# Row groups of 8 and 4 for the reversed loads, angles in turns by integer rounding, chunk C of the first batch later, and two narrower tiles, in a fused Fourier mixing and SwiGLU kernel

## The chip, the cores and the metric

The kernel runs on one core of a Trainium2 chip. The metric is the device time of one execution in microseconds (us), and the figure of a kernel is the median of its runs. Before the change it was 713.37 us in three runs (713.21 to 714.16). A program on one core has no other cores to be compared with. Its runs are called fast when they lie within 1.5% of the fastest run of the same kernel.

The engines are named as in the profile: PE is the matrix engine, PEld its weight loads, DVE the vector engine, ACT the scalar engine (activations and copies), POOL the general engine (GpSimd), and SP the queue that issues most transfers.

## The reference

```python
def _attn_ref(x):                       # x: (8, 3008, 256)
    X = np.fft.fft(x, axis=1)
    X = np.fft.fft(X, axis=2)
    return X.real.astype(np.float32)

def _moe_ref(x, w_gate, w_val, w_out):  # x: (24064, 256), weights 256 x 1536 and 1536 x 256
    g = x @ w_gate
    silu = g * (1.0 / (1.0 + np.exp(-g)))
    val = x @ w_val
    return (silu * val @ w_out).astype(np.float32)
```

The output of the first function, as 24064 rows of 256, is the input of the second.

## The kernel before

The kernel uses the symmetry of a real transform: it makes the cosine part P and the sine part Q of each batch for half of the columns, and gets one output row from P + Q and its mirror from P - Q. So the main loop has "plus halves" (`part_a`) and "minus halves" (`part_b`). A tile is up to 512 columns, a unit is one tile and one of 12 blocks of 128 hidden features, and tile t begins at unit 12t.

For each batch the input rows come in two chunks, A (128 rows) and C (60 rows and one more), each with ascending ("up") and descending ("down") rows. For batches 1 to 7 the POOL engine folds them into coefficients (`CEa`, `BBa`, `CEc`, `BBc`), and PE transforms the coefficients. The first batch is different, because PE has nothing else to do: the rows of one direction are put in order by a product with a permutation (`place`), DVE adds and subtracts (`sums`), ACT copies to bf16 (`halves`), and PE multiplies without the folds (`unfolded`). The other half of the first batch's columns, the job (0, 1), is done with folds at unit 9.

```python
    T = 512
    nT = (NC + T - 1) // T                    # NC = 8 * 1504 columns
    ...
    LA, NA = 16, P // 16                      # chunk A: 8 groups of 16 rows
    LC, NC_ = 15, NCR // 15                   # chunk C: 4 groups of 15 rows
    ...
    def up_block(b, j, n):
        return rows_at(b, 2 * j - 1, [[2 * D, n], [R * D, 4], [1, 2 * D]])
    def down_set(b, a, j, L, n):
        return rows_at(b, R * (a + 1) - 2 * j, [[2 * L * D, n], [-2 * D, L], [1, 2 * D]])
    def load_a(b, q):                         # batches 1 to 7
        X3 = XA.rearrange("p a q d -> p a (q d)")
        return ([lambda h=h: q.dma_start(out=X3[LA * h:LA * (h + 1), 0:4, :],
                                         in_=up_block(b, JA - LA * h, LA)) for h in range(NA)] +
                [lambda a=a: q.dma_start(out=X3[:, 4 + a, :], in_=down_set(b, a, JA, LA, NA)) for a in range(4)])
    ...                                       # the start; temporaries of two pools that are released together:
    SA = tp.tile([P, 2, 4, 2, D], F32, name="SA")
    SC = tq.tile([P, 2, 2, 2, D], F32, name="SC")
    ...
    psA = place(XA, putA, 4, ((psG, "g"), (psV, "v")))
    sums(SA, 0, XA, psA)
    halves(SBa, SA, 0)
    clear(XC, 1)                              # ACT
    sums(SA, 1, XA, psA)
    halves(SBa, SA, 1)
    psC = place(XC0, putC, 2, ((psO, "o"),))  # PE: waits for chunk C's rows
    unfolded(0, 0, SBa, True, False)          # PE: chunk A's products
    ...
    for q in range(2):                        # POOL: folds of the first batch, chunk A then C
        ...
            pts(dst, src, scalar1=sgn, scalar2=sg, op0=Alu.mult, op1=Alu.mult)   # BBc, the last read of SC
    ...
    transform(0, 0, (0, 1), acc)
    tmp_ctx.close()                           # all the temporaries' memory becomes free for the main loop
    hp = ctx.enter_context(tc.tile_pool(name="ht", bufs=2))
    sgp = ctx.enter_context(tc.tile_pool(name="sg", bufs=3))                     # Silu's outputs
    ...
            if k:                             # in transform_w, per block of weights
                nc.scalar.copy(dst[:, gv, fs], ps)
                nc.scalar.activation(Wm[:, gv, fs], ps, AF.Copy, scale=m2)       # ACT
```

## Time and profile before

| | before |
|---|---|
| median of three runs | 713.37 us |
| span of the profiled run | 709.6 us, PE clock 0.984 of full |
| PE busy | 672.3 us, 95% |
| POOL busy | 581.6 us, 82% |
| first product of the main loop | 39.30 us |
| start of job (0, 1), unit 9 | 65.18 us |
| start of job (2, 1), unit 76 | 224.89 us |

The page of the kernel before: its first lines, and from the slices (40 of 17.7 us; each digit is the busy share in tenths) those of PE, POOL and the PE clock.

```profile
span 709.6 us, 13046 instructions
PE 672.3 (95%) x4293; PEld 413.7 (58%) x4363; DVE 520.0 (73%) x932; ACT 439.9 (62%) x762; POOL 581.6 (82%) x563
...
PE   4678999998999999999999999999999999999997
POOL 7995889999898989999799889999699854654610
PEclk9699999999999999999999999999999999999999
```

PE is full from the fifth slice on, but for one at about 160 us. So only the start, the stretch to 200 us and the tail can give anything. The windows of the kernel before (stretch in us; its length; busy time of PE, PEld, DVE, ACT and POOL, with instructions; PE clock; share of the 16 DMA engines; GB/s):

```profile
16.00:23.70 7.70, 0.00 (x0) 0.00 (x0) 2.37 (x5) 7.62 (x5) 7.25 (x13) 0.50 0.62 115
...
58.00:62.00 4.00, 1.91 (x9) 0.68 (x7) 3.66 (x5) 1.63 (x3) 3.84 (x6) 1.00 1.10 133
...
100.00:120.00 20.00, 19.83 (x129) 12.62 (x129) 15.69 (x25) 13.23 (x24) 17.68 (x18) 1.00 0.23 77
140.00:160.00 20.00, 18.44 (x119) 11.60 (x120) 15.27 (x25) 12.65 (x22) 19.92 (x20) 1.00 0.18 57
160.00:180.00 20.00, 16.73 (x102) 9.21 (x102) 11.96 (x28) 8.38 (x15) 18.54 (x19) 0.91 0.57 137
200.00:320.00 120.00, 118.89 (x755) 72.56 (x767) 91.47 (x157) 75.77 (x133) 113.82 (x104) 1.00 0.28 73
```

From 140 to 180 us PE loses 4.8 of 40 us while POOL is busy 38.5 of 40: PE waits there for POOL's late work. The waits are 1.4 us at 159.8 for POOL's product `hp`, 0.95 us at 164.1 for a buffer `vv` that POOL frees, and 1.8 and 0.3 us at 169.7 for the coefficients of batch 2. (The profile names ACT for the 1.8 us, but POOL's `CEa` ends at 169.64, just before PE goes on.) The two longest waits of PE (waits view: engine, tile and line, what it waited for; us in all, times, longest):

```profile
PE o L380 <- ACT SBa L394: 13.9, 1, 13.9
PE o L448 <- ACT Wm L432: 3.1, 1, 3.1
```

The first is put down to ACT, but line 380 is `place`, and the tile in it is chunk C's. The timeline shows what happens (start, us, engine, line, instruction, and in brackets the idle time just before and what ended it):

```profile
23.76 3.75 PE L380 MATMUL o<-XC_106,putC 128*128 128x512 f32 x4 [13.89 <-ACT SBa L394]
39.30 0.39 PE L703 MATMUL g<-Pt,Wp 128*128 128x512 bf16 x1 [0.73 <-DVE Pt L572]
39.34 0.50 POOL L501 TENSOR_SCALAR BBc<-SC,sgn 128x1 bf16<-128x1 f32 x2
40.52 0.60 ACT L730 ACTIVATE sg<-g 128x512 f32<-128x512 f32 x1 [1.75 <-PE g L703]
73.02 4.67 POOL L148 TENSOR_TENSOR SDf<-XA 128x1024 f32<-128x1024 f32 x2 [10.32 <-DMA XA<-in_x_dram]
```

The placement of chunk C stands in PE's queue ahead of chunk A's products, and its rows come late, so PE is idle from 9.9 to 23.8 us and its clock falls to 0.50 (first window above). The Trainium skill, "TensorE: Matmul & The Clock Gate", section "What's actually happening", says that the halved clock is the default state and comes back after an idle window of about 3.4 us. The trace of this wait is compatible with that: by the same view the clock was still 1.00 from 12 to 14 us, 0.78 from 14 to 16, and 0.50 after.

### The profile page before, as it was taken

How to read it: one execution, taken by the hardware profiler on the slowest of the kernel's cores; microseconds unless marked ns; L12 is line 12 of the kernel's file. 1: busy time of each engine (PE TensorE's matmuls, PEld its weight loads, DVE VectorE, ACT ScalarE, POOL GpSimd, SP SyncE). 2: the span in 40 equal slices, each digit the busy share in tenths (PEclk: the TensorE clock that was granted, in tenths of full speed). 3: DMA queues.
4: the chain of work that ended last, by engine and by line, in shares of the span. 5: the costliest groups of instructions: out<-in, count | busy, mean ns of one | idle time of the engine just before them, and what ended most of it. 6: DMA issues, size and time to landing. Idle time of an engine off the chain costs nothing.

```text
span 709.6 us, 13046 instructions
## 1 busy us (share of the span) xinstructions
PE 672.3 (95%) x4293; PEld 413.7 (58%) x4363; DVE 520.0 (73%) x932; ACT 439.9 (62%) x762; POOL 581.6 (82%) x563
## 2 busy tenths in 40 slices
PE   4678999998999999999999999999999999999997
PEld 3333656554665656656566556656566556656686
DVE  7378667775777787777787777777877777777762
ACT  6566656563665656656666566656666566666663
POOL 7995889999898989999799889999699854654610
PEclk9699999999999999999999999999999999999999
DMA  6727471516116214206114311115211111111112
GB/s 193 137 35 133 118 161 40 135 44 149 46 45 124 71 30 108 95 30 164 31 46 87 107 31 46 45 31 124 70 46 46 30 45 31 45 45 31 46 51 70
DMA packets 44984, 52.57 MB, mean 74 GB/s; under 512 B 5676, under 2 KB 32884, under 8 KB 44916
## 3 DMA queue, kind: packets, MB, share of 16 engines
q1 hardware_dynamic: 41732, 49.38, 26.8%
q0 software_dynamic: 3184, 2.36, 2.4%
q8 instruction: 34, 0.56, 0.3%
q14 instruction: 34, 0.28, 0.1%
HBM read 29.43 MB, written 24.65 MB: 76 GB/s over the span
## 4 chain that ended last, share of the span: by engine, by line
PE 73%; POOL 8%; issue 4%; DMA 3%; DVE 3%; SPq 1%; ACT 1%; POOLq 0%; ACTq 0%
PE o L665 29%; PE v L703 15%; PE g L703 12%; PE g L740 7%; POOL SDf L148 3%; PE v L740 3%; PE g L556 3%; DMA XA<-in_x_dram 3%; PE v L556 2%; DVE vv L722 2%; POOL hp L723 1%; POOL EOf L155 1%; DMA XC<-in_x_dram 1%; DVE vv L720 1%; POOL EOf L151 1%
## 5 line engine op out<-in xcount | busy, mean ns | idle before, releaser
L723 POOL TENSOR_TENSOR hp<-sgv,vv 128x512 bf16<-128x512 f32 x126 | 161.1, 1281 | 62.5 <-DVE vv L720 46.7
L745 POOL TENSOR_TENSOR hm<-sgv,vv 128x512 bf16<-128x512 f32 x126 | 160.9, 1280 | 17.4 <-ACT sgv L744 16.1
L665 PE MATMUL o<-Wo,hp 128*128 128x256 bf16 (+1 forms) x1140 | 170.2, 273 | 2.4 <-POOL hp L723 1.4
L665 PE MATMUL o<-Wo,hm 128*128 128x256 bf16 x1128 | 168.2, 273 | 0.0
L665 PEld LDWEIGHTS <-hp 128*128 128x128 bf16 (+1 forms) x1140 | 111.4, 98 | 71.4 <-issue 9.5
L665 PEld LDWEIGHTS <-hm 128*128 128x128 bf16 x1128 | 110.2, 98 | 63.6 <-issue 3.9
L718 DVE SCALAR_TENSOR_TENSOR es<-bc,w_85,v 128x512 f32<-128x512 f32 x126 | 93.9, 746 | 55.8 <-PE v L703 55.8
L731 DVE TENSOR_TENSOR hp<-sg,v 128x512 bf16<-128x512 f32 (+1 forms) x162 | 107.7, 665 | 33.9 <-ACT sg L730 32.2
L748 ACT ACTIVATE sg<-g 128x512 f32<-128x512 f32 (+1 forms) x162 | 94.6, 584 | 47.3 <-PE g L740 44.1
L730 ACT ACTIVATE sg<-g 128x512 f32<-128x512 f32 (+1 forms) x162 | 94.3, 582 | 45.6 <-PE g L703 42.1
L749 DVE TENSOR_TENSOR hm<-sg,v 128x512 bf16<-128x512 f32 (+1 forms) x162 | 107.1, 661 | 19.8 <-ACT sg L748 11.5
L703 PE MATMUL v<-Pt,Wp 128*128 128x512 bf16 (+1 forms) x287 | 108.0, 376 | 2.7 <-issue 0.2
L703 PE MATMUL g<-Pt,Wp 128*128 128x512 bf16 (+1 forms) x287 | 108.1, 377 | 0.7 <-DVE Pt L572 0.7
L740 PE MATMUL g<-Qt,Wm 128*128 128x512 bf16 (+1 forms) x288 | 108.1, 375 | 0.0
L744 ACT ACTIVATE sgv<-g 128x512 f32<-128x512 f32 x126 | 75.5, 599 | 48.1 <-PE g L740 42.9
L715 ACT ACTIVATE sgv<-g 128x512 f32<-128x512 f32 x126 | 75.3, 597 | 43.3 <-PE g L703 16.8
L720 DVE SCALAR_TENSOR_TENSOR vv<-v,es 128x512 f32<-128x512 f32 x126 | 87.2, 692 | 18.1 <-POOL hp L723 1.5
L703 PE MATMUL g<-Qt,Wq 128*128 128x512 bf16 (+1 forms) x240 | 90.0, 375 | 0.6 <-DVE Qt L572 0.3
L722 DVE SCALAR_TENSOR_TENSOR vv<-v,es 128x512 f32<-128x512 f32 x126 | 85.9, 682 | 4.8 <-POOL hm L745 4.3
L703 PEld LDWEIGHTS <-Wp 128*128 128x128 bf16 x576 | 56.5, 98 | 45.1 <-issue 7.9
L671 ACT COPY ev<-o 128x512 f32<-128x512 f32 x94 | 55.1, 586 | 32.6 <-PE o L665 30.9
L148 POOL TENSOR_TENSOR SDf<-XA 128x1024 f32<-128x1024 f32 x28 | 66.1, 2363 | 10.4 <-DMA XA<-in_x_dram 10.3
(179 smaller groups left out, 745.4 us busy)
## 6 DMA issues: line engine op xcount, KB each, us to landing
out_dram<-ev SPq DMA_DIRECT2D x96, 128.0 KB
XA<-in_x_dram SPq DMA_DIRECT2D x32, 256.0 KB
XA<-in_x_dram SPq DMA_DIRECT2D x56, 128.0 KB
XC<-in_x_dram SPq DMA_DIRECT2D x56, 120.0 KB
XA<-in_x_dram SPq DMA_DIRECT2D x1, 1024.0 KB
out_dram<-ev SPq DMA_DIRECT2D x8, 120.0 KB
out_dram<-ev SPq DMA_DIRECT2D x8, 112.0 KB
out_dram<-ev SPq DMA_DIRECT2D x8, 104.0 KB
```

The costliest lines, as they stand in the source:

```text
L665: nc.tensor.matmul(ps[:n, j, :], hts[minus][:, f, c:c + n], Wo[:, f, :], start=(f == 0), stop=(f == nF - 1))
L703: nc.tensor.matmul(ps[:, :w], Wt[:, gv, fs], src[:, :w], start=start, stop=stop, skip_group_check=True)
L718: stt(es, bc[t], w0[:, f:f + 1], e, op0=Alu.mult, op1=Alu.add)
L720: stt(vp, o, -0.5, es, op0=Alu.mult, op1=Alu.add)
L722: stt(vm[:, ::-1], o, 0.5, es, op0=Alu.mult, op1=Alu.add)
L723: nc.gpsimd.tensor_tensor(hts[t][0][:, f, :w], sg, vp, op=Alu.mult)
L730: nc.scalar.activation(sg[:, :w], g[:, :w], AF.Silu)
L731: nc.vector.tensor_tensor(hts[t][0][:, f, :w], sg[:, :w], v[:, :w], op=Alu.mult)
L740: nc.tensor.matmul(ps[:, :w], Wm[:, gv, f * P:(f + 1) * P], Qt[:, :w], start=False, stop=True, skip_group_check=True)
L745: nc.gpsimd.tensor_tensor(hts[t][1][:, f, :], sg, v, op=Alu.mult)
L748: nc.scalar.activation(sg[:, :w], g[:, :w], AF.Silu)
L749: nc.vector.tensor_tensor(hts[t][1][:, f, w - 1::-1], sg[:, :w], v[:, :w], op=Alu.mult)
```

## The change

The intent is a shorter start, and less waiting for the folds later:

- Row groups of 8 (A) and 4 (C) in place of 16 and 15, so that the down rows of the first batch have 16 and 15 groups.
- Angles are counted in turns: POOL rounds by writing an integer, which takes away one pass per table, and some clears and weights of DVE and ACT go.
- A's products stand ahead of C's placement.
- `Wm` is made by POOL, from `Wq`, instead of by ACT.
- Tiles 0 and 3 have 480 columns, so that batches 0 and 1 end with a tile, and batch 1's and 2's transforms are needed 12 units later; the folds are spread anew.

```diff
+    wide = [H - 2 * T, T, T] * 2
+    wide += [T] * ((NC - sum(wide)) // T)
+    if sum(wide) < NC:
+        wide.append(NC - sum(wide))
...
-    LA, NA = 16, P // 16
-    LC, NC_ = 15, NCR // 15
+    LA, NA = 8, P // 8
+    LC, NC_ = 4, NCR // 4
...
     def turns(...):
-            pts(t1[:, i, :], kf[:, lo:hi], scalar1=mM[...], scalar2=BIG, op0=Alu.mult, op1=Alu.add)
-        pts(t1, t1, scalar1=-BIG, scalar2=-float(M), op0=Alu.add, op1=Alu.mult)
+            pts(t1[:, i, :], kf, scalar1=mM[...], scalar2=1.0, op0=Alu.mult, op1=Alu.mult)   # t1 is int32
...
     def weigh(lo, hi):
-        for i in range(2):
-            vts(Tab[:, 1, i, :, lo:hi], Tab[:, 1, i, :, lo:hi], scalar1=wC[:, i:i + 1], ...)
+        vts(Tab[:, 1, 1, :, lo:hi], Tab[:, 1, 1, :, lo:hi], scalar1=wC, ...)
...
-                nc.scalar.activation(Wm[:, gv, fs], ps, AF.Copy, scale=m2)
+                pts(Wm[:, gv, fs], dst[:, gv, fs], scalar1=m2, scalar2=1.0, op0=Alu.mult, op1=Alu.mult)
...
     sums(SA, 0, XA, psA)
     halves(SBa, SA, 0)
-    clear(XC, 1)
+    d_tables()
     sums(SA, 1, XA, psA)
+    unfolded(0, 0, SBa, True, False)
     halves(SBa, SA, 1)
+    ...                                    # tables of chunk C
     psC = place(XC0, putC, 2, ((psO, "o"),))
-    unfolded(0, 0, SBa, True, False)
...
-    spread(("C", 1), 14, 1, 10)
-    spread(("A", 1), 14, 11, slot[(1, 0)] - 1)
+    spread(("C", 1), 14, 1, 12)
+    spread(("A", 1), 14, 13, 24)
+    lo = 25
     for b in range(2, B, 2):
         u = slot[(b, 0)] - 1
-        lo = max(u - 43, slot[(1, 0)])
-        spread(("C", b), 14, lo, lo + (u - lo) // 2)
-        spread(("A", b), 14, lo + (u - lo) // 2 + 1, u)
-        spread(("A", b + 1), 14, u + 6, u + 28)
+        spread(("C", b), 14, lo, (lo + u) // 2)
+        spread(("A", b), 14, (lo + u) // 2 + 1, u)
+        lo = min(u + 26, slot[(b + 1, 0)] - 2)
+        spread(("A", b + 1), 14, u + 2, lo)
+        lo += 1
...
-              4: [..., lambda: value_rows((1, 2))],
+              8: [lambda: value_rows((1, 2))]}
-    for i in range(4):                     # clears of XC on DVE at units 3 to 6
-        before[3 + i].append(lambda i=i: nc.vector.memset(XC...[32:64, ...], 0.0))
...
-        if i == 5:
+        if i == 9:
             loads.extend((("A", 1), fn) for fn in load_a(1, nc.sync))
```

## The prediction

> **What bounds it now.** Page: span 709.6 us, PE busy 672.3 (95%), POOL 581.6 (82%). Stage table: from 200 to 700 us PE is busy 99 of every 100 us at clock 1.00, so only the start can give much. PE idles 16 us in 0-40 (and about 5 us of its busy time there is warm-up on zeros), 8 in 40-100, 5.4 in 100-200, 4 in the tail.
>
> Start, timeline: the placement of chunk C's rows stands in PE's queue ahead of chunk A's products; PE waits 13.9 us in one piece (9.9 to 23.8, waits view), then runs at clock 0.5. First main-loop product 39.3. Units 1-4 are bound by ACT (two 0.6 us Silu, 0.59 + 0.69 us weight copies, a 0.92 us table); PE waits 3.1 us and goes cold once more; unit 5's minus half runs at 56.8. XA for batch 1 is issued at 53.4, lands at 72.5; POOL idles 10.3 us for it. The 100-200 loss is POOL: batches 2's folds are late (waits at 159-170 us, 6 us with the cold clock after them).
>
> **Removed, moved, added.**
> - A's products, placement of C afterwards; XC0 cleared early, down rows of batch 0 in 16 and 15 row groups instead of 8 and 4. The Trainium skill, "DMA: Bandwidth & Descriptors", section "Why a DMA increments its semaphore by 16 and not by 1", says the number of engines must divide the outermost sizes; the trace agrees in kind: 378 GB/s while the one-piece up block lands, 188 after. Later batches swap the two directions, so no gain there, but 20 issues instead of 12 (0.3-0.6 us each on SP), hidden.
> - The 3.6 us clear between the halves copies leaves ACT; the rounding loses one POOL pass of 0.83 us per chunk, twice in the start and twice later.
> - Estimated from these durations: sums of A at 9 (13.6), A's products at 14 (27.3), first unit at 27.5 us (39.3): 12 us earlier.
> - But POOL now makes Wm (0.67 us each, six), and is the next limit: A's and C's remaining folds take 16 us on POOL (23.9 to 39.9) and still start at about 24.5. They end near 40.5; then Wm, two 2.35 us folds of batch 1, the second Wm at about 47. Unit 5 needs it, PE gets there near 39. I expect a PE wait of 6-8 us on POOL and a cold clock after it (about 1.7 us). Unit 5's minus half: about 47-48, so 8 us of the 12 remain.
> - Batch 1 is needed one tile later (unit 33, not 21), batch 2 at 64 instead of 52: the waits of 95 and 159-170 us should shrink (6-8 us). POOL pays: batch 3's and 4's folds are squeezed into units 65-123 (POOL need about 141 us, PE about 140), so some 3-4 us of waits may come back before batch 4 (unit 124).
> - Last tile 320 columns instead of 256: one more output block, 12 x 0.11 = 1.3 us.
>
> **Sum.** 8 + 7 - 3.5 - 1.3 = 10 us: 703.4 us, range 697.5 to 709. Faster by over 2% (below 699.1): 0.2; within 2%: 0.78; slower: 0.02.
>
> **What would show it.** A's products start near 14 us with no 13.9 us wait; first unit near 27-29; a PE wait of several us on POOL's Wm near 40-47; little PE idle at 160-175; POOL over 95% busy from 90 to 320 us; last output block train 72 products.
>
> **What would make it wrong.** Wm on POOL not stalling unit 5 (then under 699); the integer output or conversion slower on POOL; chunk C's rows landing late behind the other loads; XC of batch 2 late behind 40 issues, with POOL waiting; POOL lag from units 65-123 stalling PE by more than 5 us (then 708 or more).

## The result

| | before | after |
|---|---|---|
| median of four runs of each, same chip | 713.29 us (710.33 to 714.16) | 704.34 us (703.65 to 707.96) |
| ratio of the fast runs | | 0.9892, 95% interval 0.9848 to 0.9936 |
| span of the profiled run | 709.6 us | 702.1 us, PE clock 0.99 |

A ratio here is the mean time of one kernel's fast runs over that of the other's of the same rounds, so it is not quite the ratio of the medians quoted. The kernel is 1.1% faster. The time lies 0.9 us from the predicted one. The steps on the way to it were not all right, and that is the subject of the rest.

The page and the windows of the kernel after:

```profile
span 702.1 us, 13265 instructions
PE 676.2 (96%) x4375; PEld 415.8 (59%) x4375; DVE 513.6 (73%) x919; ACT 432.7 (62%) x759; POOL 581.0 (83%) x567
...
PE   7659998999999999999999999999999999999997
POOL 7888789999999999999998989998899645645600
PEclk9979999999999999999999999999999999999999
```

```profile
10.00:16.00 6.00, 3.39 (x12) 1.48 (x12) 5.53 (x10) 4.72 (x7) 5.83 (x11) 0.72 1.13 232
...
58.00:66.00 8.00, 8.00 (x43) 4.02 (x42) 7.14 (x15) 5.78 (x11) 7.84 (x9) 1.00 0.49 103
...
100.00:120.00 20.00, 17.37 (x117) 10.13 (x116) 13.51 (x30) 9.67 (x19) 19.27 (x17) 1.00 0.67 146
140.00:160.00 20.00, 19.90 (x133) 12.76 (x132) 15.52 (x26) 13.56 (x25) 19.92 (x19) 1.00 0.39 114
160.00:180.00 20.00, 20.00 (x133) 13.07 (x131) 14.89 (x23) 13.41 (x25) 19.92 (x20) 1.00 0.20 56
200.00:320.00 120.00, 119.63 (x769) 72.48 (x767) 90.99 (x157) 76.00 (x133) 118.03 (x110) 1.00 0.28 75
```

The loss of 140 to 180 us is gone, with POOL just as busy. A new one stands at 100 to 120 us. In the first 40 us PE has the busy first slice that was wanted, and then a hole: the second and third digits are 6 and 5. The waits of PE name it:

```profile
PE g L742 <- ACT sg L732: 11.9, 2, 10.0
PE v L705 <- DVE vv L724: 2.4, 1, 2.4
```

And the timeline of the kernel after, from the first products to the folds of batch 1:

```profile
12.26 0.50 PE L419 MATMUL v<-Tab,SBa 128*128 128x377 bf16 x1 [2.15 <-ACT SBa L394]
27.63 0.38 PE L705 MATMUL g<-Pt,Wp 128*128 128x480 bf16 x1 [1.15 <-DVE Pt L577]
40.77 0.56 PE L742 MATMUL g<-Qt,Wm 128*128 128x480 bf16 x1 [10.00 <-ACT sg L732]
53.27 0.36 PE L742 MATMUL g<-Qt,Wm 128*128 128x480 bf16 x1 [1.87 <-ACT sg L732]
...
40.15 0.57 ACT L732 ACTIVATE sg<-g 128x480 f32<-128x480 f32 x1 [13.46 <-POOL BBc L505]
...
39.61 0.50 POOL L505 TENSOR_SCALAR BBc<-SC,sgn 128x1 bf16<-128x1 f32 x2
46.83 0.69 POOL L433 TENSOR_SCALAR Wm<-Wq,m_89 128x512 bf16<-128x512 bf16 x1
74.91 4.67 POOL L152 TENSOR_TENSOR SDf<-XA 128x1024 f32<-128x1024 f32 x2 [7.56 <-DMA XC<-in_x_dram]
```

The first product of the main loop starts at 27.63 us, 11.7 us earlier, as predicted. Then nothing follows from it: the Silu of unit 0 starts at 40.15, against 40.52 before. ACT has stood idle for 13.46 us, and what ended it was POOL's `BBc` at line 505. That instruction makes coefficients of the first batch, and Silu does not read them. PE finishes the plus halves of units 0 and 1 and then waits 10.00 us.

How the gain grows and shrinks is best seen at the starts of the batches' transforms on PE (timeline), which stand at the same unit in both kernels (the expectations below call such a start the job's "anchor"):

| job, unit | before | after | gain |
|---|---|---|---|
| (0, 1), unit 9 | 65.18 | 59.95 | 5.2 |
| (1, 1), unit 40 | 136.26 | 132.56 | 3.7 |
| (2, 1), unit 76 | 224.89 | 214.29 | 10.6 |
| (4, 0), unit 124 | 335.83 | 325.22 | 10.6 |
| (7, 1) | 636.40 | 625.85 | 10.55 |
| end | 709.6 | 702.1 | 7.5 |

Part of these gains is only lent. Tiles 0 and 3 are 32 columns narrower and the last tile is 64 wider. In the timeline 512-wide products in a row start 0.215 us apart, and a tile takes about 72 of them (six in each of 12 units, a few less where blocks are split). So 32 columns make an estimate of 0.215 x 32/512 x 72 = 0.97 us per narrow tile, some 1.9 us for both, which the last tile gives back. Taking that out: the start gave about 4.5 us, the stretch to unit 40 lost 2.1, the stretch to unit 76 gave 6.3, nothing happened from there to job (7, 1), and the tail cost about 1.2 more.

### The profile page after: what moved, and what is told of

The parts are those of the page before. It is cut to its first block, busy times and chain, and to the rows that moved or that the text cites. A ratio compares the mean times of both kernels' runs of the same rounds, so it can differ in the third digit from the quotient of the medians.

```text
span 702.1 us, 13265 instructions
## 1 busy us (share of the span) xinstructions
PE 676.2 (96%) x4375; PEld 415.8 (59%) x4375; DVE 513.6 (73%) x919; ACT 432.7 (62%) x759; POOL 581.0 (83%) x567
## 4 chain that ended last, share of the span: by engine, by line
PE 89%; DVE 4%; POOL 3%; issue 2%; DMA 1%; ACT 1%; SPq 0%; DVEq 0%; ACTq 0%; POOLq 0%
PE o L667 34%; PE v L705 17%; PE g L705 16%; PE g L742 9%; PE v L742 4%; PE g L561 3%; PE v L561 3%; DVE vv L724 2%; DMA XA<-in_x_dram 1%; DVE vv L722 1%; PE g L837 1%; PE o L428 1%; PE v L419 1%; PE v L567 1%; PE g L567 1%
## 5 line engine op out<-in xcount | busy, mean ns | idle before, releaser
L725 POOL TENSOR_TENSOR hp<-sgv,vv 128x512 bf16<-128x512 f32 (+1 forms) x126 | 160.5, 1275 | 52.5 <-DVE vv L722 37.5
L747 POOL TENSOR_TENSOR hm<-sgv,vv 128x512 bf16<-128x512 f32 (+1 forms) x126 | 160.2, 1274 | 14.8 <-ACT sgv L746 14.3
L667 PE MATMUL o<-Wo,hp 128*128 128x256 bf16 (+2 forms) x1140 | 169.7, 273 | 0.0
L667 PE MATMUL o<-Wo,hm 128*128 128x256 bf16 (+2 forms) x1140 | 169.6, 273 | 0.0
L667 PEld LDWEIGHTS <-hp 128*128 128x128 bf16 (+2 forms) x1140 | 111.9, 98 | 68.1 <-issue 7.8
L667 PEld LDWEIGHTS <-hm 128*128 128x128 bf16 (+2 forms) x1140 | 111.9, 98 | 64.3 <-issue 4.4
L732 ACT ACTIVATE sg<-g 128x512 f32<-128x512 f32 (+2 forms) x162 | 94.4, 583 | 57.0 <-PE g L705 42.7
L750 ACT ACTIVATE sg<-g 128x512 f32<-128x512 f32 (+2 forms) x162 | 94.7, 584 | 44.4 <-PE g L742 43.6
L742 PE MATMUL g<-Qt,Wm 128*128 128x512 bf16 (+2 forms) x288 | 108.3, 376 | 11.9 <-ACT sg L732 11.9
L746 ACT ACTIVATE sgv<-g 128x512 f32<-128x512 f32 (+1 forms) x126 | 75.3, 598 | 48.1 <-PE g L742 38.7
L717 ACT ACTIVATE sgv<-g 128x512 f32<-128x512 f32 (+1 forms) x126 | 75.1, 596 | 43.4 <-PE g L705 34.0
L722 DVE SCALAR_TENSOR_TENSOR vv<-v,es 128x512 f32<-128x512 f32 (+1 forms) x126 | 87.0, 690 | 18.5 <-POOL hp L725 1.7
L724 DVE SCALAR_TENSOR_TENSOR vv<-v,es 128x512 f32<-128x512 f32 (+1 forms) x126 | 85.6, 679 | 6.2 <-POOL hm L747 3.3
```

Source lines behind the costliest of these rows:

```text
L667: nc.tensor.matmul(ps[:n, j, :], hts[minus][:, f, c:c + n], Wo[:, f, :], start=(f == 0), stop=(f == nF - 1))
L722: stt(vp[:, :w], o[:, :w], -0.5, es[:, :w], op0=Alu.mult, op1=Alu.add)
L724: stt(vm[:, w - 1::-1], o[:, :w], 0.5, es[:, :w], op0=Alu.mult, op1=Alu.add)
L725: nc.gpsimd.tensor_tensor(hts[t][0][:, f, :w], sg[:, :w], vp[:, :w], op=Alu.mult)
L732: nc.scalar.activation(sg[:, :w], g[:, :w], AF.Silu)
L742: nc.tensor.matmul(ps[:, :w], Wm[:, gv, f * P:(f + 1) * P], Qt[:, :w], start=False, stop=True, skip_group_check=True)
```

## The experiments

All twelve ran correctly. In every list of waits, line numbers are of that kernel (the kernels with moved memory are up to five lines longer). "After" is the kernel after, 704.34 us and ratio 0.9892. Each run's ratio is to runs of the kernel before on the same chip, whose median was 711.62, 712.52 and 712.82 us; two kernels are compared through these ratios.

The theory at the start: the Silu of unit 0 waits because its output lies in memory that was released with all the first batch's temporaries at once (`tmp_ctx.close()`), and the last reader of all these temporaries is POOL's `BBc`. The rival is the prediction's own: POOL makes `Wm` too late, and the wait on unit 0 is only where it shows.

### e1: the temporaries not in the way

`SC` and `SA` are put into memory that is not released: `SC` lies over POOL's fold buffer, which is idle then, and `SA` over the buffer of the odd tiles' products, which is used first by tile 1.

```diff
+    HT1 = const.tile([P, nF * (2 * T + B)], BF16, name="HT1")
...
-    SA = tp.tile([P, 2, 4, 2, D], F32, name="SA")
+    SA = HT1[:, 0:8192].bitcast(F32).rearrange(...)    # HT1: odd tiles' hp and hm, always there
...
-    SC = tq.tile([P, 2, 2, 2, D], F32, name="SC")
+    SC = SDf.rearrange("p k (a q) d -> p k a q d", a=2)
...
-    hp = ctx.enter_context(tc.tile_pool(name="ht", bufs=2))
+    hp = ctx.enter_context(tc.tile_pool(name="ht", bufs=1))    # even tiles only
...                                                    # part_a takes HT1 for the odd tiles
```

> Kernel after, but the two temporaries that POOL reads last (the sums of A and of C) lie in memory that is not given back before the main loop (C's in the fold buffer, A's in the second h buffer). Nothing else is changed. Theory 1: the 10 us wait of PE at unit 1 is unit 0's Silu waiting for the release of the temporaries' memory, whose last reader is POOL's BBc at 40.1 us. Then unit 0's Silu starts near 29 us (40.15 in after), the 10 us wait is gone, and the wait I forecast appears instead: unit 4's minus half waits for POOL's second Wm until 47 to 48 us (53.3 in after). Span 702.1 falls to 696-699. Rival A: what is gained at the start is given back before unit 64, because POOL's folds of batches 1 and 2 are what counts from 75 to 190 us: start as in theory 1, span 701-702.5. Rival B: the wait has another cause (PSUM, PE's queue): Silu of unit 0 stays at 40.

Measured: 703.61 us (702.93 to 704.89), ratio 0.9881 (0.9823 to 0.9939). The waits of PE, then the timeline of PE at unit 4 and of POOL at batch 1, and the window in which batch 1's load moves:

```profile
PE v L747 <- POOL Wm L434: 4.9, 1, 4.9
PE v L710 <- DVE vv L729: 4.8, 3, 2.4
```

```profile
47.30 0.58 PE L747 MATMUL v<-Qt,Wm 128*128 128x480 bf16 x1 [4.89 <-POOL Wm L434]
...
73.94 4.66 POOL L153 TENSOR_TENSOR SDf<-XA 128x1024 f32<-128x1024 f32 x2 [7.71 <-DMA out_dram<-ev]
...
52.00:60.00 8.00, 7.95 (x42) 4.07 (x42) 7.05 (x15) 5.61 (x11) 7.76 (x9) 1.00 0.47 74
```

The 10 us wait is gone: Silu of unit 0 runs at 29.10, and job (0, 1) starts at 54.31 instead of 59.95. So the release of these two temporaries was the cause of that wait, and this is shown. (Whether Silu waits for all the temporaries or only for those whose bytes it takes, e1 does not separate.) Behind it comes the wait that had been predicted, on POOL's `Wm`, until 47.30 us, the very time of the prediction ("at about 47"). In the kernel after the same `Wm` comes just as late (46.83 in its timeline), but PE is later still, so it shows as no wait.

And yet the time did not move. Job (1, 0) starts at 114.73 us, against 114.86 in after: all of the 5.6 us are given back in 60 us. POOL is idle for 7.71 us and begins to fold batch 1's chunk A at 73.94, against 74.91 in after. From there to job (1, 0) POOL is nearly full (busy 38.7 of the 40 us from 80 to 120), and PE comes to wait for it: it is busy 33.4 of these 40 us, against 37.3 in after (the longest waits are 2 us at 99 and 2.4 us at 107, on `vv`, whose buffers POOL frees).

Why does POOL start hardly earlier? The load of batch 1 was issued at 51.96 us, 5.6 us earlier than in after (57.60), but its first blocks then moved at 74 GB/s (the window above) instead of 103 (58 to 66 us in after), and so POOL got its rows only 1 us earlier. Why the same blocks moved more slowly is not known. The profile names a store, `out_dram`, as what ended POOL's wait; that it was the load is shown by e5 below.

### e2 and e3: Wm by ACT again, without and with e1

```diff
-                pts(Wm[:, gv, fs], dst[:, gv, fs], scalar1=m2, scalar2=1.0, op0=Alu.mult, op1=Alu.mult)
+                nc.scalar.activation(Wm[:, gv, fs], ps, AF.Copy, scale=m2)
```

> Kernel after, with Wm copied by ACT from PSUM as before, instead of by POOL. Theory 1: POOL's BBc ends 1.4 us earlier, so unit 0's Silu starts near 38.7 instead of 40.15; units 1 to 4 get 0.7 us longer on ACT, about 2.5 us in all, so the second PE wait is larger; net within 1.5 us of after (702.1). If Wm on POOL had been the limit that I forecast (at unit 4), the span would fall by 5 us or more.

Measured for e2: 706.8 us (704.39 to 709.88), ratio 0.9929 (0.9862 to 0.9995). So it is about 0.4% slower than after by the ratios, not faster as it would have to be if `Wm` on POOL were the limit; the difference is within the intervals of both.

> Both edits. Theory 1: no PE wait above 2 us between 28 and 60 us; unit 4's minus half at 40-43 us (53.3 in after). If only the start counts the span is about 691-693. Rival A (POOL's folds take it back by unit 64): PE waits of several us turn up between 75 and 190 us and the span is 696-700, no better than with the first edit alone.

Measured for e3, which is e1 and e2 together: 701.31 us (700.14 to 701.92), ratio 0.9844 (0.9787 to 0.9901), 2.3 us below e1 on the same chip. Job (0, 1) starts at 52.98 and job (1, 0) at 112.19, and no wait of PE on POOL's `Wm` is left.

The same edit is worth nothing, or a loss, while the release stands in the way, and a gain of 2.3 us when it does not. The rival, that `Wm` on POOL is what bounds the kernel after, falls with e2. Why e2 is rather slower is argued and not shown: when ACT may start only at about 40 us, the copies fall into the stretch where ACT has most to do.

### e5: e1 with batch 1's loads three units earlier

e1 pointed to the load. The weights' raw values lie in `XA`, and the load of batch 1 can only be queued after their last reader, `value_rows((1, 2))`, at unit 8.

```diff
               5: [lambda: weigh(NOO, NTAB)],
-              8: [lambda: value_rows((1, 2))]}
+              5: [lambda: weigh(NOO, NTAB), lambda: value_rows((1, 2))]}
-        if i == 9:
+        if i == 6:
             loads.extend((("A", 1), fn) for fn in load_a(1, nc.sync))
```

> The first edit (temporaries not given back early) and, besides, batch 1's chunk A loaded earlier: the value rows of the last two weight chunks, which hold its memory, at unit 5 instead of 8, and the loads from unit 6 instead of 9. Theory 2: in the first run the 6 us gained at the start were lost because POOL waited 7.7 us (until 73.9 us) for these loads, and its late folds then held the products of tile 2. Then POOL's wait goes, its fold of chunk A of batch 1 starts near 67 (73.9), batch 1's transform is at 108-111 instead of 114.7, and the span is 696-699. Rival A: POOL's work up to unit 64 is the limit whatever it starts with, and the span stays at 701-702.5.

Measured: 697.49 us (697.38 to 697.82), ratio 0.9779 (0.9733 to 0.9826). Job (0, 1) is where e1 has it (54.86), and job (1, 0) comes at 108.32 instead of 114.73. The fold of batch 1 in the timeline:

```profile
66.90 4.68 POOL L153 TENSOR_TENSOR SDf<-XA 128x1024 f32<-128x1024 f32 x2 [0.39 <-POOL BBc L172]
```

POOL now goes from chunk C to chunk A without a gap, 7.0 us earlier than in e1, and all or nearly all of it reaches the end (6.1 us by the medians, 6.4 by the profiled spans, about 7 by the ratios). So the gain of e1 had been lost to POOL's wait for batch 1's load, and this too is shown.

### e11: the earlier loads alone

> The kernel after with only the earlier loads of batch 1 (issued from unit 6, the memory they go to freed at unit 5), no memory moved. e5 against e1 gave 6.1 us for this step when unit 0 was not held. If POOL's idle time before batch 1 (7.56 us) is what counts and it starts from the load: loads issued near 52 to 54 instead of 57.6, POOL idle 3 to 5 us, anchor of (1,0) 3 to 4 us earlier (111 to 112), time 700 to 702. If the two steps only pay together: within 1 us of after (703.5 to 705).

Measured: 700.84 us (700.16 to 701.91), ratio 0.9834 (0.9801 to 0.9867). Job (1, 0) starts at 111.12, and POOL's gap is 3.68 us instead of 7.56. Against after, by the ratios, e1 alone gives about 0.8 us, e11 alone 4.1, and both (e5) 8.1 (by the medians, 0.7, 3.5 and 6.9). The intervals are 2 to 4 us wide to each side, so the times alone do not show that the two are worth more together than apart; job (1, 0) shows it, which comes 0.1, 3.7 and 6.5 us earlier than in after. They help each other: freeing unit 0 moves PE forward, and that is kept only if POOL's work comes forward as well.

### e8 and e12: all three, and one thing more

e8 is e3 with the loads of e5.

> All three edits: temporaries kept, Wm on ACT, loads from unit 6. Theory 2: against the run with the first two (699.9) POOL's wait for batch 1's loads goes and the span falls by 3-6 us to 694-697; batch 1's transform at 106-109 (112.2). Rival A: span 699-700.

Measured: 695.47 us (694.4 to 695.68), ratio 0.9748 (0.9709 to 0.9788): faster by over 2%, and the best with e12. Job (0, 1) starts at 52.44, (1, 0) at 105.84, (2, 0) at 176.82.

e12 is e8 without the split blocks in tile 2. A split block makes plus and minus halves on POOL and saves PE a product.

```diff
-        return 2 <= u[0] < nT - 1 and u[1] in SPLIT
+        return 3 <= u[0] < nT - 1 and u[1] in SPLIT
```

> e8 with tile 2 not split into plus and minus halves in the split blocks, which takes about 15 us of work off POOL in units 24 to 35 and adds about 1.3 us of PE products. If POOL is still the limit around 80 to 120 us (PE waits on DVE vv and on hp there): the waits at 97 to 112 go, anchor of (1,0) 2 to 4 us earlier than e8's 105.84, (2,0) at 173 to 176 against 176.82, time 692 to 694.5 against 695.5. If it is the load of batch 1 alone: 695.5 to 697.

Measured: 695.0 us (694.12 to 696.56), ratio 0.9753 (0.972 to 0.9786). That is e8's time. The windows of 80 to 120 us show PE busy 39.76 us instead of 38.53, so 1.2 us of waiting did go. The products that were added were reckoned at 1.3 us, and job (2, 0) starts at 177.95, later than e8's 176.82. The guess that POOL's load was still worth 2 to 4 us there was wrong.

### e7, e9 and e10: what the row groups are worth

e7 is after with the old row groups, and nothing else.

```diff
-    LA, NA = 8, P // 8
-    LC, NC_ = 4, NCR // 4
+    LA, NA = 16, P // 16
+    LC, NC_ = 15, NCR // 15
```

> Kernel after with the row blocks of before (16 and 15). Theory: batch 0's down rows come over 8 and 4 engines instead of 16 and 15, the sums of A end 2-3 us later, and with them the first unit (29.5-30.5 instead of 27.6) and POOL's BBc (42 instead of 40.1); loads of batch 1 take as long as in after, since up and down rows change places; span 703-705. Rival: fewer load issues (12 and 18 instead of 20 and 40) bring the loads of batches 1 and 2 sooner and the span falls below 701.

Measured: 721.3 us (719.83 to 723.33), ratio 1.0116 (1.0071 to 1.016), slower than before the change and about 16 us slower than after by the ratios. The timeline of its start:

```profile
17.76 0.50 PE L419 MATMUL v<-Tab,SBa 128*128 128x377 bf16 x1 [7.18 <-ACT SBa L394]
29.63 3.75 PE L381 MATMUL o<-XC,putC 128*128 128x512 f32 x4 [6.04 <-issue]
42.53 0.38 PE L705 MATMUL g<-Pt,Wp 128*128 128x480 bf16 x1 [1.14 <-DVE Pt L577]
```

A's products come 5.5 us later than in after, C's placement 12.8 us later (16.81 there), and the main loop 14.9 us later; then the release costs 10 us as well. So in the new order the row groups are worth 14.9 us at the first unit, far more than had been expected, and without them the main loop would start later than before the change (39.30). The prediction had given its 12 us to the order, the clear and the loads together, without a figure for each.

e9 is the other way round: the kernel before with the new row groups, in the old order.

> The kernel before with one edit: row groups of 8 and 4 in place of 16 and 15 for the down rows, in the old order. Theory R (the rows are worth much only in the new order, where A's and C's products wait for their own rows; in the old order everything waits for the same last load): XC0 is placed near 17 to 18 us instead of 23.76, the first unit's product near 33 to 35 instead of 39.30, but the Silu of unit 0 stays at 39 to 41 us, since POOL's last BBc fold (39.84) releases the temporaries; anchor of (0,1) within 1.5 us of 65.18, time within 2 us of the kernel before. Rival S (the rows are worth their 18 us of e7 in any order): first unit below 31, time 6 us or more below before.

Measured: 710.58 us (710.5 to 710.63), ratio 0.997 (0.9932 to 1.0007). Its timeline:

```profile
15.19 3.75 PE L380 MATMUL o<-XC,putC 128*128 128x512 f32 x4 [5.42 <-DMA XC<-in_x_dram]
31.37 0.39 PE L703 MATMUL g<-Pt,Wp 128*128 128x512 bf16 x1 [0.73 <-DVE Pt L572]
39.70 0.60 ACT L730 ACTIVATE sg<-g 128x512 f32<-128x512 f32 x1 [8.87 <-POOL BBc L501]
```

The rows of C come 8.6 us earlier and the main loop 7.9 us earlier, more than expected. Silu of unit 0 stays at 39.70 as expected, held by POOL's `BBc`, and job (0, 1) starts at 65.06 against 65.18. So the release held unit 0 in the old program too, as a limit just behind the visible one: a main loop that starts 7.9 us earlier was worth nothing by job (0, 1). That it was not the only limit there is seen in e10.

e9 shows one thing more. POOL's fold of batch 1's chunk A starts at 69.84 us, 3.2 us earlier than before the change (73.02), after a wait of 7.26 us that a transfer ended:

```profile
69.84 4.68 POOL L148 TENSOR_TENSOR SDf<-XA 128x1024 f32<-128x1024 f32 x2 [7.26 <-DMA XC<-in_x_dram]
```

The load was issued at 52.06 instead of 53.39 us, and from the issue to the fold it took 17.8 us instead of 19.6. So the new row groups do not slow the load of batch 1 as a whole.

e10 is e9 with the memory of e1.

> e9 with the two temporaries moved out of the way as in e1, so that unit 0's Silu does not wait for POOL's folds. If the release is what held e9: Silu of unit 0 follows its products directly (near 34 to 36), anchor of (0,1) 3 to 5 us earlier than in e9, and some of that kept: time 2 to 4 us below e9. If the release is not a limit in the old order: within 1 us of e9.

Measured: runs of 711.68, 711.07, 703.53 and 703.49 us, ratio 0.9925 (0.9859 to 0.9991). These are two levels, and the profiled run is of the slow one, so the time settles nothing; what separates the levels stays open, as no trace of a 703.5 us run exists. The profiled run shows one thing. Silu of unit 0 runs at 33.98, and still job (0, 1) starts at 64.86, as in e9 and before. The timeline says why:

```profile
47.82 0.57 PE L449 MATMUL o<-SDt,XA 128*128 128x1 bf16 x16 [4.72 <-ACT Wm L433]
...
51.87 4.36 DVE L314 TENSOR_SCALAR Tab<-Tab,wC 128x752 bf16<-128x752 bf16 x2
...
58.16 0.59 PE L745 MATMUL v<-Qt,Wm 128*128 128x512 bf16 x1 [3.65 <-DVE hp L736]
```

In the old program ACT and DVE are the next limits. PE first waits 4.72 us for ACT's `Wm`, which stands in ACT's queue behind a table for which ACT itself had waited 2.78 us for DVE. Then DVE weighs both tables (4.36 us) and clears `XC` in four pieces of 0.91 us between the units, and PE waits 3.65 us behind that. The change takes `Wm` from ACT, cuts the weighing to one table and takes the clears out. So in this stretch several limits lie close behind each other. That removing the release, with the new rows, gains nothing by job (0, 1) is shown; that DVE's and ACT's work is the whole reason is read from the waits, and no run tests it.

### e4 and e6: the old tiles

e6 is after with tiles of 512 and, as near as the program allows, the old schedule of the folds (e4 is a first attempt at it).

```diff
-    wide = [H - 2 * T, T, T] * 2
+    wide = []
...
-    spread(("A", 1), 14, 13, 24)
+    spread(("A", 1), 14, 13, slot[(1, 0)] - 1)
...  # and the old loop for the batches from 2 on; in e4 chunk C of batch 1 also at units 1 to 10
```

> Kernel after with the tile widths of before (23 tiles of 512, then 256) and with the fold schedule of before that belongs to them. Theory: the PE waits before batch 2's transform (5-7 us with the cold clock, at 150-175 us) come back, the tail is 1.3 us shorter: span 706-709. Rival: the waits at 160-175 of before came from its late start of the folds alone, and the start of after is enough to remove them: span 701-703.

Measured for e4: 730.62 us (729.05 to 735.52), ratio 1.0283 (1.0213 to 1.0353). This is no test of the tiles. Chunk C's folds ended earlier, so the loads of the next C were queued ahead of batch 1's A; POOL waited 20.4 us for it, to 87.7 us, and PE 9.5 and 8.4 us for `CEa`. What the run shows is only that the order of the load queue is worth as much as the whole change.

> The old tile widths again, now with the loads in their order: in the run that failed, chunk C of batches 2 and 3 had got ahead of batch 1's chunk A (POOL waited 20 us for it). Chunk C of batch 1 is folded in units 1-12, chunk A in 13-20, the rest as before. Theory: batch 1's transform at unit 21 waits for POOL (A's folds end near 97, PE is there near 87): waits of 5-10 us at 85-97, and again 3-6 us before batch 2 at 155-175; span 707-713. Rival: 701-703, widths do not matter.

Measured for e6: 718.81 us (718.21 to 719.17), ratio 1.0078 (1.0037 to 1.0118), about 13 us above after by the ratios. The waits of PE:

```profile
PE g L742 <- ACT sg L732: 12.2, 3, 10.1
PE g L561 <- POOL CEa L165: 8.3, 1, 8.3
```

```profile
96.68 0.34 PE L561 MATMUL g<-Tab,CEa 128*128 128x189 bf16 x1 [8.35 <-POOL CEa L165]
```

The first is the release, as in after. The second is job (1, 0), which stands at unit 21 with the old tiles: PE begins it at 87.74 us, when POOL has folded only the first half of batch 1's chunk A, and from about 88.3 to 96.68 us it waits for the coefficients of the second half. (POOL had itself waited 9.1 us for batch 1's load.) With the new tiles the same job is at unit 33. So with this start the new tiles and the new spread together are worth about 13 us; how much is due to each was not separated.

## Why the prediction was right in the time and wrong on the way

The predicted 703.4 us and the measured 704.34 differ by 0.9 us, but the gains compare more exactly: the sum predicted 10 us, and the profiled span fell by 7.5 (709.6 to 702.1; the ratio of the fast runs, 0.9892, gives 7.7). Of the gains the "measured" column has the lent 1.9 us of the narrower tiles taken out.

| term of the prediction | predicted | measured |
|---|---|---|
| start, to unit 9 | +8 | +4.5 |
| later waits (95 us, 159 to 170 us) | +7 | +6.3 - 2.1 = +4.2 |
| POOL lag before batch 4 | -3.5 | 0 |
| tail block | -1.3 | about -1.2 |
| sum | +10 | +7.5 |

**The start up to the first unit: right.** "A's products at 14 (27.3), first unit at 27.5 us (39.3)": 12.26 and 27.63 us. The 13.9 us wait is gone.

**The start after the first unit: the step that failed.** "I expect a PE wait of 6-8 us on POOL and a cold clock after it (about 1.7 us). Unit 5's minus half: about 47-48, so 8 us of the 12 remain." The minus half in question (unit 4 when the first is called 0; it stood at 56.78 us before) runs at 53.27 us, so 3.5 us remain of the 12. The wait was on POOL, but not for `Wm`, and it came at unit 0. The Silu of unit 0 writes to memory that is given out anew only when temporaries are released, and their last reader is POOL's fold, which ends at 40.1 us. The prediction had the end of that fold right ("near 40.5") and did not ask what else waits for it. e1 shows both: take the release away and the wait is gone, and the predicted wait on `Wm` appears, 4.89 us long (6 to 8 had been predicted), to 47.30. The prediction's mechanism was real, and hidden behind another.

**Later waits: direction right, size too large.** PE's loss at 140 to 180 us went from 4.8 to 0.1 us, as predicted. But the prediction counted the wait of about 95 us as gained too, and the stretch of 80 to 120 us got worse (PE busy 37.3 us instead of 38.9): POOL begins batch 1's chunk A at 74.91 instead of 73.02 us, and PE loses 2.6 us in 100 to 120. e5 and e11 show that batch 1's load is the cause: queued three units earlier, it gives back about 4 us alone and 7 us on top of e1, by the ratios.

**"Later batches swap the two directions, so no gain there": right in kind.** By the pattern in `load_a`, up blocks of 8 rows have an outermost size of 8, and down sets have 16. The Trainium skill, "DMA: Bandwidth & Descriptors", section "Why a DMA increments its semaphore by 16 and not by 1", says that a transfer uses the largest number of engines up to 16 that divides the slowest sizes of both sides. The windows agree: the up blocks of batch 1 move with a DMA share of 0.49 and 103 GB/s after (58 to 66 us), against 1.10 and 133 GB/s before (58 to 62). But these are the up blocks alone. From the issue of its first block to POOL's first fold the whole load took 17.3 us after and 19.6 before (17.8 in e9, where only the row groups are new), so a cost of the swap is not seen. That POOL starts on batch 1 1.9 us later than before goes with the later issue of the load (57.60 instead of 53.39 us). In the first batch the gain is large, and e9 shows it without any other change: C's rows are placed at 15.19 instead of 23.76 us.

**POOL lag before batch 4: wrong.** POOL is busy 79.69 of the 80 us from 260 to 340 after, which is the predicted fullness, but PE's gain is 10.6 us at job (2, 1) as well as at job (4, 0). Here POOL was full and still in time, and it cost nothing.

**Tail: right.** The products with `hm` are 1140 instead of 1128, one block more; about 3 us of gain go between job (7, 1) and the end, of which the wider tile takes 1.9 by the estimate above.

So two errors of about 3.5 us, one in each direction, met in the sum, which is luck, and the lost 2.8 us of the later waits are most of what is left.

What stays open: the two levels of e10, why batch 1's up blocks moved at 74 GB/s in e1 and at 103 in after, and which part of e7's 16 us belongs to chunk A's groups and which to C's. The best kernels measured are e8 and e12, at 695 us and ratios of 0.9748 and 0.9753, and e8 differs from the kernel after only by where two temporaries lie, by which engine makes `Wm`, and by three units in the issue of one load (with the value rows that free its memory).

## What to carry to other kernels

When a start is made shorter, list for the first instructions of the next stage everything that they wait for, the release of memory too: temporaries that are freed together can hold the next stage until their slowest reader is done, and as long as another wait ends later this doesn't show in the profile. Limits that were just behind the bottleneck come forward one after the other (here the rows, the release, `Wm`, the load of batch 1), so test the parts in combination: the edit of `Wm` gained nothing alone and 2.3 us with another. And a sum that hits the time is no proof of its terms; measure the gain at several points of the program.

## What the Trainium skill lacked or had wrong

- "DMA: Bandwidth & Descriptors" had nothing wrong here: what it states of the number of engines agrees with the share of the up blocks of batch 1 (0.49 with 8 rows to a block, 1.10 with 16).
- No page has the wait, an instruction held until the last reader of released temporaries is done, and how to find it in a trace: ACT idle for 13.46 us, ended by a POOL instruction whose output the ACT instruction does not read.
- "TensorE: Matmul & The Clock Gate" has the clock fall after at least one idle window of about 3.4 us. Before the change it fell about 5 us after the last product, which fits (1.00 until 15.0 us in a wait that began at 9.9). In the kernel after it fell about 2.1 us after the last product (0.50 from 12.25 us on in a wait that began at 10.1), which does not. The measurement decides; why the clock fell so soon is not known.
